# A new table of places for the backward recurrence of a memory transformer on one core

## The chip, the cores and the metric

The kernel runs on one core of one Trainium2 chip. The metric is the time of one execution on the device in microseconds (us). Three runs of the kernel before gave 2830.5, 2833.98 and 2844.75 us; the median, 2833.98, is the time to compare with. The engines are named as in the profile: PE (TensorE, matmuls; PEld is its weight load), DVE (VectorE), ACT (ScalarE), POOL (GpSimd) and SP, on whose queue all transfers of the stage concerned are issued.

## The reference

The forward pass is a layer norm, then the sum of the input, an attention whose memory of 8 rows is carried from one segment of 32 tokens to the next, and an MLP with a squared ReLU. The kernel computes the output and the gradients of all ten tensors for a given gradient of the output.

```python
B, S, Dm = (1, 2048, 512)
H, Dh = (32, 128)
M, seg = (8, 32)
...
for s in range(n_seg):
    xs = x[:, s * seg_len:(s + 1) * seg_len, :].copy()
    h = jnp.concatenate([mem, xs], axis=1)
    q = jnp.einsum('btd,dhe->bhte', h, Wq)
    k = jnp.einsum('btd,dhe->bhte', h, Wk)
    v = jnp.einsum('btd,dhe->bhte', h, Wv)
    scores = jnp.einsum('bhqe,bhke->bhqk', q, k) * scale
    scores = jnp.where(mask[None, None], scores, -1000000000.0)
    p = _softmax(scores, axis=-1)
    o = jnp.einsum('bhqk,bhke->bhqe', p, v)
    o = jnp.einsum('bhte,hed->btd', o, Wo)
    mem = o[:, :M, :].copy()
    outs.append(o[:, M:, :])
...
return x + _A_ref(xn, A_mem0, A_Wq, A_Wk, A_Wv, A_Wo, A_seg_len) + _B_ref(xn, B_w1, B_b1, B_w2, B_b2)
...
_out, _vjp = jax.vjp(_f, A_x, A_mem0, A_Wq, A_Wk, A_Wv, A_Wo, B_w1, B_b1, B_w2, B_b2)
_grads = _vjp(grad_out)
return (_out0, *[jnp.asarray(_g) for _g in _grads])
```

There are 64 segments, each of which needs the memory of the one before; in the backward pass each needs the gradient of the memory of the one after.

## The kernel before

The program has the stages forward recurrence, MLP, backward recurrence (the second recurrence, L1705 to L2078) and weight gradients (L2162). Only the second recurrence is touched. It walks the 64 segments from the last to the first, in 16 blocks of four; the segments of a block are called 3, 2, 1 and 0, and are done in that order.

**One segment's chain** (`chain`, L1920). The gradient of the memory comes from R_A, the sum for this segment's input rows. R_A is evicted from PSUM in two halves (L1980 states them, L763 is an eviction on DVE, L765 one on ACT; in the trace R_A is an XN of 128x256, f32). The matmul **gm** (L1992) picks the memory rows out of it, and a copy on DVE (L1995) puts them into the matrix gT. Then **gO**, the projection by the output weights (L873, four parts gO00, gO01, gO10, gO11), its eviction, its transposes **gOT** (L759) and their eviction, and **dP** (L1937), the gradient of the probabilities, in two halves. On DVE the softmax backward follows, for each half four operations (L1958, L1960, L1961, L1963) and transposes (L1967, L1968). Small copies fill block-diagonal matrices from its results (L999; BDA, BDB and XK in the trace), on ACT, DVE or POOL. With these PE does the **bd** matmuls (L983; bd2, bd1 and bd0 for v, k and q, each in two halves), each half is evicted (L765 or L763, into XK), transposed on DVE (L856), and multiplied by the weights (**dR2, dR1, dR0**, L1777, four steps each) into R_A for the segment before. The evicted gradients, dN, also go to memory (S_GN, three stores of 256 KB per segment); dN2 and dN0 share one buffer, so the next one is evicted after the store has read it.

**Filler.** Between the steps of the chain PE does work of neighbouring blocks that does not hang on the chain: `l_pre` (L1788) prepares the next block's local part (gL and dp, and pre.dg at L939, and a softmax on DVE, L1760 to L1765), and `l_post` (L1826) finishes the last block's: post.own (L1864), post.mm (L1877) and dRL (24 steps of L1777, with XN as input). gNat (L2013) are transposes of gT after a block is done.

**What sets the order.** Nothing is scheduled when the kernel is built. `_Beat.run` (L573) pops the operations from a heap as soon as those they depend on are out. The key is a number from a table plus a fixed beat for each block; the remainder of the number by 4 names the engine, for the copies that several engines can do:

```python
x = own[1 if o.blk == 0 else 2 if o.blk == self.last else 0][o.slot]
e = ("PE", "ACT", "DVE", "POOL")[x % 4] if len(o.cost) > 1 else next(iter(o.cost))
heapq.heappush(heap, (self.beat * o.blk + x // 4, o.idx, e))
...
_, i, e = heapq.heappop(heap)
seq.append((self.ops[i], e))
```

There are three tables in `_BWD` (L197): for the 14 middle blocks, for the first and for the last block. Each engine, and SP's queue, does its instructions in the order in which they come off the heap. A place is only an order; a transfer or an engine that is late makes those behind it wait.

Of the kernel before, what the change touches and what calls it, by code (L numbers as in the profile page):

```python
# [205 lines left out]
        -546000, -2857200, -480000, -481200, -46343678, 1958400, 3563600, 3428400, 3358800, -39445799, -3474280,  # L206
        -1361679, 2911440, -5698598, 6099600, 4994800, 2060400, 541200, 4580802, 7385202, 7385602, 8326802, 8824402,
        9103200, 9060400, 12611600, 12610400, 6769762, -57689959, -4334000, -3086798, -8438400, -12837600, -319597,
        -13471197, -16186000, 938000, 7771520, 7770320, 7974082, -12147880, -36138158, 8458960, 7771680, -8353800,
        -31747319, 8462400, -36193079, 9695640, -50492597, -69540277, -42304997, -47596277, 5526803, -19093437,  # L210
        -6835677, -4532037, 8168480, -52982319, 8492560, -35859039, 8101002, 8275242, 9959080, -11536760, 2676160,
        -6802360, -5640120, 8030522, 8029322, 8640522, 11057002, 11480802, 11054602, 11479602, 11169682, 11053402,
        11052202, 11166082, 12529242, 13047722, 11577282, -53185477, -47912717, -46746037, -35873437, -26574079,
        -41158999, -3076599, -21554757, 11212360, -21629439, -6090039, 11539522, 7252481, -6895997, -8092680,
        -17924919, 12833482, 13066282, 12876240, 12875040, 12828880, 12873840, 14037400, -57547477, -18138439,
        -21536557, -24487719, 11602322, -46193917, 11601122, -40852157, -10002840, 13779282, -43878718, 11390242,
        -39385558, -10128439, -12102397, -45351999, -12199997, -9629117, 12830080, 13828081, -1848078, -8506838,
        12332320, 12331120, 12380240, 12380240, -37160200, 14192521, 14713641, 2556960, -5265118, 1378880, -58560038,
        9791040, -36825960, 23496720, -26575120, 3544040, -30169437, 10715403, 14217080, -2427160, -21531640,
        -24941080, -26533360, -965320, -9348360, -4744280, -2117080, -9645557, -4299440, -4982320, -4689600, -3734720,  # L220
        -45051079, 1432880, -190760, 143640, 170960, -12251559, 4149840, 4316040, 4314840, 4313640, -444838, -2435878,
        4726002, 5218242, -314198, 6272960, 6271760, 6140240, 6422880, -13898000, 15057720, 15056520, -78482159,
        15704400, -31640798, 16583800, 15669280, 15668080, -31651159, 16441160, 4105522, 17918400, -44856717,
        -49497237, 12097443, 14069203, 15760843, -13303037, -24924477, 14658563, -1036080, -12120519, 16517640,
        -12171479, -19164078, 16333722, 18497320, 18496120, 18374600, 18373400, -16882000, -7618398, 19291482,
        8963202, -1006558, 7859002, -10244638, -8975838, 19549882, -19454878, -2022158, -22659278, 4534722, 17929402,
        -18420838, -4276997, 10220123, -15301237, 16219523, -28146359, -10193797, -48781357, -18599357, 18309560,
        -23528479, -13879038, -7373558, -10161077, -9652838, 19720960, -4986318, 19557922, 16324922, 20802000,
        20800800, 21247800, 21246600, 20708240, -48823239, -5933437, -20262439, -26219437, -700039, -18122837,
        -19469237, -21622759, 18592960, 19820441, -17140839, -38326879, -20258439, -24316917, -15836677, -9607317,  # L230
        10993321, -19470397, 20806200, -9618559, -2440598, 10800642, 20664920, 20663720, 21187560, 19381040, 9514760,
        -31648438, -51401599, 21992720, 6632762, 21999880, 19977762, 14024000, 11239960, 23859600, -49781320,
        -27474160, 11856363, 5703803, -13820320, -23800120, 22382040, 20342520, -21640039, 22438800, -18114918,
        22528840, 22438280, 22171720, 8096121, 22699840, -20694919, 23625560, 12662283, -30947157, 14340323,
        -31376917, 12732363, 20788683, -20774837, -9932197, 22519320, -5755239, 22616720, -4144719, 13732122,
        21493322, 24284480, 24289280, 24279680, 24286880, 710240, 12368682, 12608882, 16282482, 23172642, 23649362,
        18415762, 23257962, 21492122, 23472122, 23038122, 23036922, 20708242, 23650562, 24117602, -10181877, 15361043,
        -45284197, -5213277, -28628559, 11584403, -18779559, 16282521, 24308840, 4772161, 11541603, 7885001, 21513123,
        9730121, 24352920, 4695441, 22456642, 23126042, 25675960, 25672360, 26009600, 25617680, 8765280, 12337841,
        -14024677, -21028397, -14720079, 5575883, 23280602, 23322362, 14584721, 24369440, 22963802, 8381161, 8379961,  # L240
        2859121, 18921401, 25701003, 23965202, 13830203, 23373882, 25671160, 10999201, 16305242, 25052002, 26008400,
        25669960, 25668760, 25868480, 16157920, 12553281, 10227922, 26094160, -18057118, 26108720, -31954518,
        26951160, -20195520, 14049520, -22449760, -3877280, 26096323, 15608603, 21197560, 10032720, 26241320,
        26237720, -19414239, 26281240, 26771362, -19806600, 26280720, 26279520, 11529081, 26799680, 20066961,
        28507720, 12895563, 10136643, 21059483, 21141563, 26591123, 7004643, 22356883, 6439723, 22656520, 11629001,
        24627920, 20068161, 25696402, 25018762, 28743680, 28743680, 28742480, 29779680, -42422640, 11044042, 16305082,
        27921522, 27538322, 29068802, 24650882, 6776522, 26190882, 16313322, 19375402, 11190962, 29320522, 16274042,
        11238882, 25372323, 20587803, 9815123, -48383117, 19292523, 3013201, 11530761, 19745083, 29055200, -32040879,
        16256721, -18660637, -21773197, -4282917, 30337920, 13860201, 29354602, 29326002, 31079640, 29877760,
        32090560, 31697440, 12144000, 13033521, -14471839, 1277843, -14338079, -9612957, -10090479, -21864637,  # L250
        -21541959, 30830320, 22919881, 3768961, 13666041, 1722803, 27275443, 18430083, 14474482, 20602681, 7341881,
        31157240, 13824001, 29362442, 19648322, 32088160, 32091760, 32086960, 32088160, 12960080, 26104721, 4714882,
# [129 lines left out]
_BWD_BEAT = 6498400  # L382
# [1842 lines left out]
```

## Time and profile before

| what | us |
| --- | --- |
| median of three runs | 2833.98 |
| lowest and highest run | 2830.5 and 2844.75 |
| span of the profiled execution | 2847.0 |
| first block of the second recurrence, 1209.5 to 1285.0 | 75.5 |
| fourteen middle blocks, 1285.0 to 2208.0 | 923.0, or 65.9 each |
| last block, 2208.2 to 2274.7 | 66.5 |
| tail, up to the weight gradients | 17.0 |

The profiled execution has one number here, its span from the first instruction to the last; that span is 13 us above the median and 2 us above the highest of the three runs. Parts of it are therefore to be compared with the span, and not with the median. The stretches of the stage are read off the trace where the first gO of a block starts.

A row of waits reads "engine line <- releaser: us in all, times, longest". A row of the timeline gives start, length, engine, line, operation, output and input, count, and in brackets the idle time before it with what ended it. In a row of a table of stretches there stand the busy time and the number of instructions of each engine, PE's granted clock (1.00 is full), the share of busy transfer engines and GB/s.

### The profile page before, as it was taken

The numbers are of one execution on the slowest core, as the hardware profiler recorded it, in microseconds if no ns is written. First come the engines' busy times: TensorE is split into PE (matmuls) and PEld (weight loads), VectorE is DVE, ScalarE is ACT, GpSimd is POOL, SyncE is SP. The second block draws the span as 40 slices with busy tenths as digits, with TensorE's granted clock in tenths as the row PEclk, the third lists the DMA queues.
The fourth block names the chain that finished last, engine by engine and source line by source line (L and its number), as shares of the span: only waits on it lengthen the run. The fifth ranks groups of instructions, "written<-read, shape, count | busy, mean of one in ns | idle before, by whom it ended". The sixth has DMA issues, their size and how long they took to land.

```text
span 2847.0 us, 114405 instructions
## 1 busy us (share of the span) xinstructions
PE 2708.2 (95%) x47681; PEld 1558.6 (55%) x47681; DVE 1630.3 (57%) x4762; ACT 1191.0 (42%) x2804; POOL 935.3 (33%) x2605
## 2 busy tenths in 40 slices
PE   9999999999999999889998999999999899999999
PEld 7665556566565565655555555555555544444444
DVE  5555666666666567776676666666676502232322
ACT  4334445555555455565554555554554400000000
POOL 1103233223333233344454444444444301111211
PEclk9999999999999999999999999999999999999999
DMA  7648677787777764568898898888888799788861
GB/s 222 208 151 239 190 195 199 211 211 203 208 206 205 194 192 161 147 163 227 224 235 217 219 228 237 221 224 223 227 220 210 224 353 295 229 254 268 254 184 42
DMA packets 556394, 606.28 MB, mean 213 GB/s; under 512 B 228145, under 2 KB 357442, under 8 KB 553826
## 3 DMA queue, kind: packets, MB, share of 16 engines
q1 hardware_dynamic: 540706, 544.88, 70.0%
q0 software_dynamic: 15168, 54.08, 6.1%
q8 instruction: 374, 6.13, 0.9%
q14 instruction: 146, 1.20, 0.1%
HBM read 290.14 MB, written 272.12 MB: 197 GB/s over the span
## 4 chain that ended last, share of the span: by engine, by line
PE 62%; DVE 12%; issue 11%; DMA 7%; ACT 3%; POOL 2%; SPq 2%; DVEq 0%; POOLq 0%; ACTq 0%
PE ps L873 16%; PE ps L2162 10%; PE ps L1777 8%; PE ps L983 5%; PE ps L759 4%; PE ps L1442 4%; PE ps_h L1183 3%; DMA S_GN<-XK 3%; PE ps L1655 3%; PE ps_B L1211 2%; PE ps_gxb L1211 2%; DVE maskA L1963 1%; SPq L819 1%; DVE XN L856 1%; ACT XK L765 1%
## 5 line engine op out<-in xcount | busy, mean ns | idle before, releaser
L873 PE MATMUL ps<-WA,PA 128*32 128x512 bf16 x6144 | 370.8, 380 | 5.3 <-DVE PA L1603 3.8
L2162 PE MATMUL ps<-WA,WB 128*128 128x512 bf16 x1536 | 332.3, 379 | 0.6 <-DVE gwo L763 0.6
L1777 PE MATMUL ps<-WA,XK 128*32 128x512 bf16 x5120 | 315.6, 381 | 9.7 <-DVE XK L856 6.2
L873 PEld LDWEIGHTS <-PA 128*32 128x32 bf16 x8192 | 208.3, 96 | 196.4 <-issue 11.3
L2162 PEld LDWEIGHTS <-WB 128*128 128x128 bf16 x1896 | 185.5, 98 | 224.5 <-issue 0.8
L999 POOL COPY BDA<-PB 32x128 bf16<-32x128 bf16 x468 | 134.9, 288 | 487.3 <-DVE PLp L1571 182.0
L763 DVE CAST gwo<-ps 128x512 bf16<-128x512 f32 x64 | 40.0, 682 | 400.3 <-PE ps L2162 268.3
L765 ACT CAST gwo<-ps 128x512 bf16<-128x512 f32 x64 | 33.1, 599 | 517.2 <-PE ps L2162 357.9
L765 ACT CAST XK<-ps 128x512 bf16<-128x512 f32 x330 | 189.5, 585 | 106.0 <-PE ps L983 61.3
L1777 PEld LDWEIGHTS <-XK 128*32 128x32 bf16 x5120 | 124.6, 97 | 144.9 <-DVE XK L856 36.3
L1777 PE MATMUL ps<-WA,XN 128*32 128x512 bf16 x2560 | 166.1, 385 | 5.9 <-DVE XN L856 5.4
L2173 POOL DMA_DIRECT2D out_dram<-gwo x96 | 71.4, 751 | 295.9 <-ACT gwo L765 264.9
L763 DVE COPY XN<-ps 128x512 bf16<-128x512 bf16 (+1 forms) x146 | 65.7, 450 | 156.5 <-PE ps L759 104.5
L765 ACT CAST XA<-ps 128x512 bf16<-128x512 f32 x141 | 82.8, 587 | 141.7 <-PE ps L873 121.3
L999 ACT COPY BDA<-PB 32x128 bf16<-32x128 bf16 x452 | 133.4, 295 | 14.3 <-DVE PB L1967 2.0
L1442 PE MATMUL ps<-WB,OT 128*32 128x256 bf16 x4096 | 130.7, 275 | 6.7 <-DVE mxA L1577 3.9
L1655 PE MATMUL ps<-XA 128*128 128x512 bf16 x448 | 133.3, 382 | 1.9 <-issue 1.9
L873 PE MATMUL ps<-WB,PA 128*32 128x512 bf16 x2048 | 126.2, 384 | 6.4 <-issue 5.2
L765 ACT COPY XN<-ps 128x256 f32<-128x256 f32 (+2 forms) x158 | 73.9, 480 | 136.5 <-DVE XN L763 75.3
L983 PEld LDWEIGHTS <-XK 128*128 128x128 bf16 x1536 | 94.2, 98 | 61.5 <-POOL XK L999 26.1
L856 DVE STREAM_TRANSPOSE XK<-XK 128x256 f32<-128x256 f32 x256 | 108.7, 436 | 31.8 <-ACT XK L765 28.2
L1005 POOL COPY BDA<-XA 32x256 bf16<-32x256 bf16 x256 | 105.8, 413 | 59.7 <-PE ps L983 34.3
(309 smaller groups left out, 5555.5 us busy)
## 6 DMA issues: line engine op xcount, KB each, us to landing
S_GN<-XK SPq DMA_DIRECT2D x192, 256.0 KB
WA<-S_GN SPq DMA_DIRECT2D x160, 256.0 KB
S_K<-kN SPq DMA_DIRECT2D x64, 256.0 KB
S_Q<-qN SPq DMA_DIRECT2D x64, 256.0 KB
S_V<-vN SPq DMA_DIRECT2D x64, 256.0 KB
S_ON<-oN SPq DMA_DIRECT2D x64, 256.0 KB
XA<-S_Q SPq DMA_DIRECT2D x64, 256.0 KB
XA<-S_K SPq DMA_DIRECT2D x64, 256.0 KB
```

The lines of the kernel that those rows point to most:

```text
L759: nc.tensor.transpose(ps_ap, in_ap, ident[base:base + k, base:base + k])
L765: nc.scalar.copy(out, in_)
L856: self.plan.add({"DVE": 0.36}, lambda e, x=x: nc.vector.transpose(dst[:, x, :, :].rearrange("p i c r -> p (i c r)").bitcast(F32).rearrange ...
L873: nc.tensor.matmul(bk()[32 * j:32 * (j + 1), :], lhsT=win(dc), rhs=Wt(dc, c0), start=(dc == 0), stop=(dc == DC - 1), tile_position=(0, 32 ...
L983: nc.tensor.matmul(bv()[:, n * P:(n + 1) * P], lhsT=B_[:, i, :, :].rearrange("p j k -> p (j k)"), rhs=X[:, i, :], start=(y == 0 and n == 0 ...
L999: self.plan.add({"ACT": 0.31, "DVE": 0.2, "POOL": 0.31}, lambda e, j=j: {"ACT": nc.scalar.copy, "DVE": nc.vector.tensor_copy, "POOL": nc.g ...
L1005: self.plan.add(cost or {"ACT": 0.4, "DVE": 0.27, "POOL": 0.42}, lambda e, j=j: {"ACT": nc.scalar.copy, "DVE": nc.vector.tensor_copy, "POO ...
L1211: nc.tensor.matmul(bk()[:], lhsT=src[z][:, fc, rc * P:(rc + 1) * P], rhs=Wt[:, fc, :], start=(fc == 0 and first), stop=(fc == FC - 1))
L1442: nc.tensor.matmul(bk()[32 * t:32 * (t + 1), :], lhsT=tq(OTt, i, j), rhs=Wo[:, JQ * i + j, h * HB:(h + 1) * HB], start=(i == 0 and j < 2), ...
L1655: A(pe(0.217, "f", 0.11), lambda e, c=c, z=z, x=x: nc.tensor.matmul(bks[x]()[:], lhsT=anT[x][:, c, :], rhs=sx[z][:], start=(c == 0), stop= ...
L1777: nc.tensor.matmul(bk()[32 * j:32 * (j + 1), :], lhsT=tq(XT, i, j), rhs=wtf(t, i, j), start=(first and i == 0), stop=(last and i == NI - 1 ...
L2162: nc.tensor.matmul(bks[n]()[:], lhsT=HNc[:, rc, dc * P:(dc + 1) * P], rhs=half_of(gns[y], hf), start=(y == 0), stop=(y == NRC - 1))
```

## The change

Numbers of the three tables of `_BWD` are replaced: 550 of the 724 for the middle blocks and all of the first block's 618 and the last block's 561. The beat goes from 6498400 to 6498399. No code and no table of the forward recurrence is touched. The new numbers come from a search whose replay serves the packets of all transfers in the order of issue. What shows in a program is another order on the five engines and other engines for some copies: of the copies, evictions and casts, DVE has 1462 (1655 before), ACT 2641 (2464) and POOL 2233 (2217). Matmuls and transfers are the same ones. The new file is one line shorter, so each line behind the table has a number lower by one.

```diff
@@ -203,183 +203,182 @@
         11817202, 10472800, 15851602, -17692400, -106800, -10764000, 216000, -12492400, 3623200, 6284000, -528797,
-        -546000, -2857200, -480000, -481200, -46343678, 1958400, 3563600, 3428400, 3358800, -39445799, -3474280,
...
-_BWD_BEAT = 6498400
+_BWD_BEAT = 6498399
```

Three places show what moves. The first is DVE in segment 3 of a middle block, from the end of the first half's softmax backward to the first fill of BDB after the second half's (maskA is the result, PB its transpose). Before:

```order
L1963 SCALAR_TENSOR_TENSOR maskA<-XA 128x160
L1967 STREAM_TRANSPOSE PB<-maskA 128x128
L1958 TENSOR_TENSOR XA<-ps,XA 128x160
L1960 TENSOR_REDUCE brA<-XA 128x4
L1961 TENSOR_TENSOR XA<-ps,brA 128x160
L1963 SCALAR_TENSOR_TENSOR maskA<-XA 128x160
L1966 COPY PB<-maskA 128x4x8
L1968 STREAM_TRANSPOSE PB<-PB 128x128
L999 COPY BDB<-maskA 32x4x32
```

And with the change:

```order
L1962 SCALAR_TENSOR_TENSOR maskA<-XA 128x160
L1965 COPY PB<-maskA 128x4x8
L1966 STREAM_TRANSPOSE PB<-maskA 128x128
L1967 STREAM_TRANSPOSE PB<-PB 128x128
L855 STREAM_TRANSPOSE XN_2675<-XK_2673 128x256
L1957 TENSOR_TENSOR XA<-ps,XA 128x160
L1959 TENSOR_REDUCE brA<-XA 128x4
L1960 TENSOR_TENSOR XA<-ps,brA 128x160
L1962 SCALAR_TENSOR_TENSOR maskA<-XA 128x160
L1966 STREAM_TRANSPOSE PB<-maskA 128x128
L998 COPY BDB<-maskA 32x4x32 x2
```

The copy and transpose of the first half (L1966 and L1968 of before) moved ahead of the second half's softmax, the transpose at L1967 for the second half ahead of the fills, and DVE fills two parts of BDB instead of one. On PE in the same segment, dR2's first two steps went ahead of the second dP, its last two and bd0's first half between the two halves of bd1, and the transposes of gNat behind the first dP. The eviction of gNat went from DVE to ACT.

The second place is PE around gm, in segment 1 of a middle block. XN is here the input of dRL (filler), XK_2673 that of dR0 (the chain), PA the gT that gO reads. Before:

```order
L1777 LDWEIGHTS XN_2678
L1777 MATMUL ps<-WA,XN_2678 32x512
L1992 MATMUL ps<-sel_97,XN_2677 32x8 x16
L1777 LDWEIGHTS XN_2678
L1777 MATMUL ps<-WA,XN_2678 32x512
```

With the change:

```order
L1776 LDWEIGHTS XK_2673
L1776 MATMUL ps<-WA,XK_2673 32x512
L1991 MATMUL ps<-sel_97,XN_2677 32x8 x16
L872 LDWEIGHTS PA
L872 MATMUL ps<-WB,PA 32x512
```

The filler before gm and behind it is gone in this segment and in segment 2: gm stands right behind the last step of dR0, and gO right behind gm. In segments 3 and 0 there is still filler ahead of gm. Both evictions of R_A are ACT's in every segment now; before, DVE did 45 of them.

The third place is SP's queue, from late in segment 1 to early in segment 0 of a middle block; XK_2673 is the buffer of dN, S_V, S_VM and S_VL are loaded transposed, XA, S_Q and S_K belong to the loads of q and k. Before:

```order
L819 DMA S_GN<-XK_2673 128x1024
L819 DMA XA<-S_Q 128x1024
L1784 DMA_TRANSPOSE XK_2672<-S_VM 128x8x128
L819 DMA XA<-S_K 128x1024
L819 DMA S_GN<-XK_2673 128x1024
L1784 DMA_TRANSPOSE XA<-S_V 128x8x128
L1784 DMA_TRANSPOSE XK_2672<-S_VL 128x8x128
L819 DMA S_RL<-XN_2682 128x512
L819 DMA S_GON<-XA 128x1024
L819 DMA S_GN<-XK_2673 128x1024
```

With the change:

```order
L818 DMA XA<-S_Q 128x1024
L818 DMA XA<-S_K 128x1024
L818 DMA S_GN<-XK_2673 128x1024
L1783 DMA_TRANSPOSE XA<-S_V 128x8x128
L818 DMA S_GN<-XK_2673 128x1024
L818 DMA S_R<-XN_2677 128x512
L818 DMA S_RL<-XN_2682 128x512
L818 DMA S_GON<-XA 128x1024
L818 DMA S_GN<-XK_2673 128x1024
```

Before, the first S_GN row is dN1 of segment 1, the second dN0 of segment 1 and the third dN2 of segment 0, which needs the buffer of that dN0. With the change dN0 is stored first and dN1 behind it; the transposed load of S_VM went into segment 2 and that of S_VL further away.

338 rows, old and new, of the table _BWD are left out of this document.

## The prediction

> **What bounds the kernel now.** First the page: the span, and who is busy in it.
>
> ```profile
> span 2847.0 us, 114405 instructions
> PE 2708.2 (95%) x47681; PEld 1558.6 (55%) x47681; DVE 1630.3 (57%) x4762; ACT 1191.0 (42%) x2804; POOL 935.3 (33%) x2605
> ```
>
> PE is busy for 95% of the span, so a change of order alone can win at most PE's idle time, and only that of the stage it touches. The change touches the second recurrence. The table by stretches gives its four parts: first block, fourteen middle blocks, last block, and the tail up to the weight gradients.
>
> ```profile
> core 0: us, PE busy (x) PEld busy (x) DVE busy (x) ACT busy (x) POOL busy (x), PEclk, DMA share, GB/s
> 1209.50:1285.00 75.50, 67.22 (x1488) 43.28 (x1480) 52.40 (x142) 44.00 (x91) 33.78 (x102) 1.00 0.63 167
> 1285.00:2208.00 923.00, 857.87 (x19422) 493.82 (x19424) 610.82 (x1828) 491.05 (x1182) 437.50 (x1358) 0.99 0.87 224
> 2208.20:2274.70 66.50, 59.63 (x1239) 33.77 (x1232) 40.22 (x126) 31.64 (x78) 28.03 (x89) 0.97 0.73 214
> 2274.70:2291.70 17.00, 13.00 (x203) 6.69 (x201) 2.35 (x5) 2.23 (x4) 0.00 (x0) 0.90 0.91 304
> ```
>
> Span less PE's busy time: 8.3 us idle in the first block, 65.1 in the middle (4.65 per block), 6.9 in the last, 4.0 in the tail: 84 us in all. DVE, ACT and POOL are busy for 66%, 53% and 47% of the middle, so none of them is the bound; what counts is how late one result comes. The waits of PE in the middle say which:
>
> ```profile
> engine line waited for: us in total, times, longest us
> PE ps L983 <- DVE BDB L999: 13.0, 15, 1.3
> PE ps L1937 <- ACT XN L765: 7.0, 6, 2.4
> PE ps L873 <- issue: 5.5, 6, 1.4
> PE ps L1777 <- DVE XN L856: 5.4, 6, 1.9
> PE ps L983 <- issue: 4.3, 4, 2.1
> PE ps L983 <- POOL XK L999: 4.3, 13, 0.3
> PE ps L1777 <- DVE XK L856: 3.4, 16, 0.5
> ...
> PE ps L1992 <- ACT XN L765: 0.4, 1, 0.4
> ```
>
> Some 20 of the 65 us are "issue" (the two rows above and smaller ones): pauses that wait for nothing that is shown, which I take as untouched. About 36 us wait on an engine and can be moved. Four rows carry my sum: 13.0, 7.0, 5.4 and 4.3.
>
> **The change part by part.** No instruction of PE and no transfer is added or removed; about 190 copies go from DVE to ACT. So every term is a wait that goes, shrinks or appears.
>
> *The 13.0 us, once per block, in segment 3.* PE stands before the second half of the bd1 matmuls until DVE has filled BDB:
>
> ```profile
> 1687.52 0.86 PE L1877 MATMUL ps<-XN,XN 128*32 128x128 bf16 x32
> 1687.75 0.28 DVE L1958 TENSOR_TENSOR XA<-ps,XA 128x160 f32<-128x160 f32 x1
> 1688.54 0.39 PE L983 MATMUL ps<-XA,BDB 128*128 128x128 bf16 x4
> 1688.76 0.39 PE L983 MATMUL ps<-bqLN,XK 128*128 128x128 bf16 x4
> 1689.71 0.18 DVE L999 COPY BDB<-maskA 32x128 bf16<-32x128 bf16 x1
> 1690.04 0.38 PE L983 MATMUL ps<-XA,BDB 128*128 128x128 bf16 x4 [0.90 <-DVE BDB L999]
> ```
>
> DVE's second softmax half starts at 1687.75 and its fill ends at 1689.89. What decides is how much PE work lies between the first dP and this matmul. Four matmuls of a bd take 0.22 (the two groups that start at 1688.54 and 1688.76), so a half of bd takes 0.45; 16 of post.mm take 0.43 (half of 0.86); 16 of dR2 take 1.04 (row below). Before, what lies there is gOT1, bd2's second half, post.own, dP 1, dR2 (four steps), post.mm twice, bd1's first half and 0.22 of its second. Changed, all this and besides it bd0's first half (0.45) and the transposes of gNat (four matmuls, 0.22 by the same row): 0.7 more, against a mean wait of 13.0/14 = 0.93. DVE does not get there earlier: the eviction of gNat leaves it, a transpose and one more fill of BDB (0.18) come in, as the rows of the order show. Bounds: +2.5 (only the extra fill counts, 14 x 0.18) and -13.0. I take 14 x 0.7 = **-9.8**. What is late next there is bd0's second half, behind POOL.
>
> *The 7.0 us.* One of these six waits, in segment 0, with the ACT work that leads to it, and the row of all such waits of ACT:
>
> ```profile
> 1799.22 1.07 ACT L765 CAST XK<-ps 128x512 bf16<-128x512 f32 x2 [2.62 <-DMA S_GN<-XK]
> 1800.18 0.60 ACT L765 COPY XN<-ps 128x512 bf16<-128x512 bf16 x1
> 1800.84 0.28 PE L1937 MATMUL ps<-XA,XN 128*32 128x40 bf16 x16 [1.48 <-ACT XN L765]
> ...
> ACT XK L765 <- DMA S_GN<-XK: 27.1, 20, 3.1
> ```
>
> ACT stood for 2.62 us before an eviction into XK, because the store of the segment before (S_GN) was still reading that buffer; the eviction of gOT queued behind it, and PE behind that. In the change the store in question goes out ahead of the other store and of two transposed loads. Bounds: +2.6 (one more wait like the one shown) and -7.0; I take three quarters, **-5.3**. The 5.4 us at L1777 <- DVE XN L856 stand behind DVE's transpose of what such an eviction leaves, mostly in segment 2; there l_post's dRL steps now lie around the second dP as cover: 0 to -5.4, half, **-2.7**. The 4.3 us at L983 <- POOL: fewer fills of segment 3 stand behind POOL's copies of V (L1911); 0 to -4.3, half, **-2.1**. Together -19.9.
>
> *New: R_A uncovered.* In segments 2 and 1 no PE work is left between the last dR0 and gm (the rows of the order in the section above). R_A must first be evicted. Two places show it, covered and uncovered:
>
> ```profile
> 1266.76 0.65 ACT L765 COPY XN<-ps 128x256 f32<-128x256 f32 x2 [1.73 <-PE ps L1777]
> 1266.85 0.69 DVE L1763 TENSOR_TENSOR XN<-ps,brL 128x512 f32<-128x512 f32 x1
> 1267.19 0.59 PE L1992 MATMUL ps<-sel,XN 128*32 128x8 f32 x32 [0.46 <-ACT XN L765]
> ...
> 1727.88 1.04 PE L1777 MATMUL ps<-WA,XN 128*32 128x512 bf16 x16
> 1728.10 0.42 DVE L763 COPY XN<-ps 128x256 f32<-128x256 f32 x1 [1.61 <-PE ps L1777]
> 1728.56 0.37 ACT L765 COPY XN<-ps 128x256 f32<-128x256 f32 x1 [2.55 <-DVE XN L763]
> 1728.98 0.44 PE L1992 MATMUL ps<-sel,XN 128*32 128x8 f32 x32
> ```
>
> Below, in segment 1 of a middle block, 16 matmuls of l_post (1.04) cover both halves of the eviction and gm does not wait. Above, in the first block, nothing covers and PE idles 0.46. The first block's other gm waited up to 0.9 (rows further down). Two per block, 28 in all: bounds 28 x 0.2 = 5.6 (if ACT is free at once and the first half suffices for the first matmuls) and 28 x 0.9 = 25.2. I take the row itself, 28 x 0.46 = **+12.9**.
>
> Both halves now go to ACT, and the rows show that this loses nothing: DVE's half ended at 1728.52, ACT's began at 1728.56. If the two could run side by side, taking DVE away would cost one more 0.37 at each of the 28 uncovered places, 10.4 us; by the rows it costs 0. The Trainium skill ("PSUM — Partial Sum Buffer", section "PSUM bank collisions raise a hardware error ⚠️") says that software has to keep two engines apart on the same bank, which would put the halves one behind the other whoever copies; the trace agrees, with 0.04 us between them.
>
> *New: less between gO and its transposes.* In segments 1 and 0, gOT0 now follows gO10 directly; gO11 comes after it.
>
> ```profile
> 1332.89 1.85 PE ps L873 x32
> ...
> 1730.69 0.59 ACT L765 CAST XA<-ps 128x512 bf16<-128x512 f32 x1 [1.76 <-PE ps L873]
> ```
>
> A quarter of gO takes 1.85/4 = 0.46; the eviction before the transposes 0.59, so PE lacks 0.13 and what the hand-over takes, 0.2 by my estimate (0.04 lies between the two halves of R_A above). Bounds 0.1 and 0.4; 28 x 0.2 = **+5.6**. In segment 0, dR1's third step now precedes bd0's second half and needs a transpose that DVE does behind one softmax step of l_pre (0.69 at L1763): 0 to 0.69, nearest to the middle since two steps of dR1 (1.04, as for dR2) still cover: 14 x 0.3 = **+4.2**. Together +22.7.
>
> Middle blocks: -19.9 + 22.7 = +2.8.
>
> *First and last block* have their own tables.
>
> ```profile
> PE ps L1992 <- ACT XN L765: 1.4, 2, 0.9
> PE ps L983 <- DVE BDB L999: 1.0, 2, 0.8
> ...
> PE ps L1992 <- DVE XN L763: 0.9, 1, 0.9
> ...
> PE ps L1937 <- ACT XN L765: 2.8, 1, 2.8
> PE ps L1877 <- DMA XN<-S_DSL: 2.4, 2, 1.9
> ```
>
> The first three are the first block's. There gm gets l_pre's and l_post's work as cover in segment 0, and gO and dP move up: of 1.4 + 1.0 + 0.9 = 3.3 and the small ones of its 8.3 us I take -4 (0 to -6). In the last block l_post's dRL steps move in beside segment 0, which covers the 2.8 us: -3 (0 to -5). The 2.4 us in the tail wait for a load behind the last store and stay.
>
> **Sum**: 2.8 - 4 - 3 = -4.2 us. The profiled execution spans 2847.0 us, 13 above the median of 2834.0 (runs 2830.5 to 2844.75), so its own result would be 2842.8; carried to the median, **2829.8**.
>
> **Rivals.** *A: the covers hold and the new gaps are small.* All four rows go (13.0 + 7.0 + 5.4 + 4.3 = 29.7), gm costs 0.2 a time, gOT 0.1, dR1 nothing: 5.6 + 2.8 = 8.4. With -7 for the ends: -28.3, 2805.7. For it: 13 us of the gain are one regular wait, and the cover fits. Against: the filler that pays for it stood before gm.
>
> *B: slower, through ACT's queue.* ACT carries both halves of R_A in every segment and gets twelve copies more per block; where one eviction of another chain (0.59) stands ahead of R_A, gm waits 0.46 + 0.59 = 1.05. That is 28 x 0.59 = 16.5 beyond the forecast, and the 5.3 taken off dP's wait are lost with it, since dP waits for ACT too: -4.2 + 21.8 = +17.6, 2851.6. Up to a wait of 0.61 at gm the kernel gains (4.2/28 = 0.15 above 0.46); from 0.93 on it is slower by what can be measured (14.2 + 4.2 - 5.3 = 13.1, 0.47 a time). For it: the first block's 0.9. Against: ACT is busy for 53% only.
>
> *C: the transfers do not keep the order of issue*, so that the new places of the S_GN stores, chosen for such an order, gain nothing: the 5.3 and 2.7 fall away, -4.2 + 8.0 = +3.8, 2837.8. For it: the row of 27.1 us shows 20 waits of ACT for stores of one size, issued by one queue, at places that differ from block to block, up to 3.1. The Trainium skill speaks for C: "DMA: Bandwidth & Descriptors", section "Two DMAs through the same engine are not ordered", has it that descriptors of one queue start in order but are pipelined, and that nothing orders transfers across the 16 engines. No row here shows two transfers overtaking each other.
>
> **How the numbers follow.** Forecast 0.38, A 0.30, C 0.12, B 0.20. About 0.5% (14.2 us: 2819.8 and 2848.2) is what a measurement of this kernel can tell from no change. Faster: A's 0.28 and 0.08 of the forecast's lower side, 0.36. Slower: B's 0.17 and 0.04 of the forecast's and C's upper side, 0.21. Same: 0.43. The forecast's own range is 2817 to 2843; to hold 8 in 10 the range runs into A and B, from 2802 to 2852.
>
> **What would show it.** In the profile after: "L983 <- DVE BDB" of the middle near 3 (right) or above 8 (wrong); "L1992 <- ACT XN" about 13, below 6 for A, above 25 for B; "L1937 <- ACT XN" below 3, or still 7 for C; "L759 <- ACT XA" new with about 5; idle of PE in the first block about 4 and in the last about 4. The prediction fails if the pauses named "issue" change, or if a late load (GON, loaded late for l_post) stops PE for whole microseconds in every block.

## The result, and the profile after

The changed kernel takes 2800.18 us (median of five runs, 2798.07 to 2812.79), the kernel before 2837.44 us (five runs, 2830.5 to 2844.75): a ratio of 0.9866, with a 95% interval from 0.9835 to 0.9897. It is faster by 1.3%, where the forecast was 2829.8 and no difference that can be told; 2800.18 lies just below the range of the forecast, 2802 to 2852.

The head of the page of the profiled execution after the change:

```profile
span 2811.0 us, 114204 instructions
PE 2701.3 (96%) x47681; PEld 1555.9 (55%) x47681; DVE 1532.6 (55%) x4569; ACT 1259.3 (45%) x2981; POOL 937.5 (33%) x2621
```

The span is 36.0 us shorter. To see where, the same stretch is cut out of both: from the first gm of segment 3 of the second block to that of the last block, which are fourteen blocks. The rows of the table by stretches are, in this order, of before, of the change, and of the change profiled a second time (columns: stretch, length, busy time of PE, PEld, DVE, ACT and POOL with counts, PE's clock, share of busy transfer engines, GB/s):

```profile
1299.70:2222.60 922.90, 858.47 (x19436) 494.26 (x19432) 611.23 (x1826) 491.20 (x1184) 437.50 (x1358) 0.99 0.87 224
1293.70:2186.60 892.90, 851.38 (x19360) 493.82 (x19356) 523.88 (x1655) 551.73 (x1345) 438.29 (x1364) 0.99 0.94 232
1286.40:2174.30 887.90, 849.34 (x19363) 493.96 (x19359) 523.66 (x1655) 551.72 (x1345) 438.24 (x1364) 1.00 0.94 233
```

The fourteen blocks are shorter by 30.0 us (922.9 to 892.9), 2.1 us per block. PE is idle in them for 41.5 us instead of 64.4, and its busy time is 7.1 us less, but this stretch also holds 76 matmuls fewer with the change, since some filler lies on the other side of the cut. The whole stage, from the last matmuls of one line late in the forward recurrence (L1554 before, L1553 after) to the end of the tail, has the same number in both:

```profile
1171.40:2291.70 1120.30, 1030.25 (x22976) 605.61 (x22969) 738.73 (x2165) 590.98 (x1389) 516.01 (x1585) 0.99 0.84 218
1165.30:2256.00 1090.70, 1026.18 (x22976) 604.97 (x22969) 640.42 (x1972) 658.30 (x1566) 518.68 (x1602) 0.99 0.90 225
```

It is shorter by 29.6 us, of which PE's busy time gives 4.1. The other 6 us of the span lie ahead of the stage, where nothing was changed: it starts at 1171.4 us before and 1165.3 after. First and last block give nothing, as the same table shows for the first block, the last and the tail of the change (75.5, 66.5 and 17.0 us before):

```profile
1200.80:1274.90 74.10, 69.87 (x1549) 44.40 (x1548) 47.67 (x131) 45.82 (x96) 35.78 (x111) 0.99 0.64 172
...
2171.00:2237.00 66.00, 62.03 (x1243) 34.18 (x1239) 34.48 (x113) 35.16 (x84) 29.55 (x96) 0.97 0.77 231
2237.00:2256.00 19.00, 11.98 (x206) 5.80 (x206) 1.78 (x4) 2.15 (x4) 0.00 (x0) 0.83 0.82 241
```

The waits of PE in the stretch of the change, and the row of ACT's waits for the stores of dN:

```profile
engine line waited for: us in total, times, longest us
PE ps L1991 <- ACT XN L764: 13.4, 28, 0.5
PE ps L1991 <- issue: 8.5, 7, 2.5
PE ps L872 <- issue: 3.4, 4, 1.9
PE ps L872 <- DVE PA L1994: 3.2, 18, 0.2
...
PE ps L1776 <- DVE XK L855: 2.1, 3, 1.3
...
ACT XK L764 <- DMA S_GN<-XK: 6.4, 7, 2.1
```

The wait of bd1 for BDB (13.0, or 12.2 in this stretch) is gone, and so is that of dP for ACT (7.0). gm (L1991) waits 28 times, 0.48 each. ACT's wait for S_GN fell from 27.1 to 6.4.

What had been in the trace of before, and was overlooked, is in segment 3 of a middle block. The timeline of before shows the segment's first dP, and POOL's copy of V beside the last step of the softmax backward of the first half; then follow, of the change, the first dP, that step of both halves, the fill of BDB, the matmul that needs it, and the copy:

```profile
1684.14 0.28 PE L1937 MATMUL ps<-XA,XN 128*32 128x40 bf16 x16
1686.20 1.03 POOL L1911 COPY XA<-XA 128x1024 bf16<-128x1024 bf16 x1
1686.47 0.94 DVE L1963 SCALAR_TENSOR_TENSOR maskA<-XA 128x160 bf16<-128x160 f32 x1
...
1664.11 0.28 PE L1936 MATMUL ps<-XA,XN 128*32 128x40 bf16 x16
1665.85 0.33 DVE L1962 SCALAR_TENSOR_TENSOR maskA<-XA 128x160 bf16<-128x160 f32 x1
1668.75 0.33 DVE L1962 SCALAR_TENSOR_TENSOR maskA<-XA 128x160 bf16<-128x160 f32 x1
1669.41 0.34 DVE L998 COPY BDB<-maskA 32x128 bf16<-32x128 bf16 x2
1670.16 0.39 PE L982 MATMUL ps<-XA,BDB 128*128 128x128 bf16 x4
1674.83 1.03 POOL L1910 COPY XA<-XA 128x1024 bf16<-128x1024 bf16 x1
```

The same instruction took 0.94 us beside the copy and takes 0.33 without it. The change has the copy 14.9 us after the segment's first gO, where it stood 4.9 us after it. That is not what took the wait away, though. The second half's fill ends 5.64 us after the first dP with the change (1664.11 to 1669.75) and ended 5.75 after it before (1684.14 to 1689.89): the step is shorter by 0.61, but DVE now has more to do ahead of the fill. It is PE that comes later, 6.05 us after the first dP, where it stood ready after 5.0 (1690.04 less the wait of 0.90). The medians of the fourteen blocks are the same: fill 5.76 before and 5.65 with the change, PE ready 5.01 and 6.05.

### The profile page after: what moved, and what is told of

Read it like the earlier page. It is cut to its first block, busy times and chain, and to the rows that moved or that the text cites. A ratio compares the mean times of both kernels' runs of the same rounds, so it can differ in the third digit from the quotient of the medians.

```text
span 2811.0 us, 114204 instructions
## 1 busy us (share of the span) xinstructions
PE 2701.3 (96%) x47681; PEld 1555.9 (55%) x47681; DVE 1532.6 (55%) x4569; ACT 1259.3 (45%) x2981; POOL 937.5 (33%) x2621
## 4 chain that ended last, share of the span: by engine, by line
PE 63%; issue 8%; DMA 4%; DVE 4%; ACT 2%; POOL 1%; SPq 0%; DVEq 0%; POOLq 0%; ACTq 0%
PE ps L872 14%; PE ps L1776 14%; PE ps L2161 12%; PE ps L982 7%; PE ps L758 4%; PE ps L1441 3%; PE ps L1654 2%; PE ps L1991 1%; PE ps L1876 1%; PE ps L938 1%; ACT XN L764 1%; PE ps L1936 1%; DMA S_GN<-XK 1%; DMA WA<-S_GN 1%; PE ps L1598 1%
## 5 line engine op out<-in xcount | busy, mean ns | idle before, releaser
L872 PE MATMUL ps<-WA,PA 128*32 128x512 bf16 x6144 | 371.1, 381 | 4.8 <-DVE PA L1602 3.8
L998 POOL COPY BDA<-PB 32x128 bf16<-32x128 bf16 x546 | 157.4, 288 | 490.3 <-DVE PLp L1570 198.1
L872 PEld LDWEIGHTS <-PA 128*32 128x32 bf16 x8192 | 206.2, 97 | 190.1 <-DVE PA L1994 12.0
L1776 PE MATMUL ps<-WA,XK 128*32 128x512 bf16 x5120 | 306.5, 382 | 4.0 <-DVE XK L855 3.9
L764 ACT CAST XK<-ps 128x512 bf16<-128x512 f32 x379 | 210.6, 589 | 80.5 <-PE ps L982 67.6
L1776 PE MATMUL ps<-WA,XN 128*32 128x512 bf16 x2560 | 173.3, 381 | 3.7 <-DVE XN L855 3.4
L764 ACT COPY XN<-ps 128x256 f32<-128x256 f32 (+2 forms) x229 | 102.2, 475 | 128.2 <-PE ps L1776 125.3
L872 PE MATMUL ps<-WB,PA 128*32 128x512 bf16 x2048 | 135.4, 389 | 8.0 <-issue 3.6
L1441 PEld LDWEIGHTS <-OT 128*32 128x32 bf16 x4096 | 102.2, 97 | 35.3 <-DVE OT L855 19.4
L1004 POOL COPY XK<-XH 32x64 bf16<-32x64 bf16 x256 | 59.5, 232 | 182.0 <-PE ps L982 171.1
```

What stands on the lines that cost most here:

```text
L764: nc.scalar.copy(out, in_)
L872: nc.tensor.matmul(bk()[32 * j:32 * (j + 1), :], lhsT=win(dc), rhs=Wt(dc, c0), start=(dc == 0), stop=(dc == DC - 1), tile_position=(0, 32 ...
L998: self.plan.add({"ACT": 0.31, "DVE": 0.2, "POOL": 0.31}, lambda e, j=j: {"ACT": nc.scalar.copy, "DVE": nc.vector.tensor_copy, "POOL": nc.g ...
L1004: self.plan.add(cost or {"ACT": 0.4, "DVE": 0.27, "POOL": 0.42}, lambda e, j=j: {"ACT": nc.scalar.copy, "DVE": nc.vector.tensor_copy, "POO ...
L1441: nc.tensor.matmul(bk()[32 * t:32 * (t + 1), :], lhsT=tq(OTt, i, j), rhs=Wo[:, JQ * i + j, h * HB:(h + 1) * HB], start=(i == 0 and j < 2), ...
L1776: nc.tensor.matmul(bk()[32 * j:32 * (j + 1), :], lhsT=tq(XT, i, j), rhs=wtf(t, i, j), start=(first and i == 0), stop=(last and i == NI - 1 ...
```

## The experiments

All times are compared with runs of the kernel before on the same chip. The stretch of fourteen blocks is cut as above. It holds pauses of PE that wait for nothing shown ("issue"), which differ from one execution to the next; the last column leaves them out, and so compares profiles better than the length does. What it still holds is the clock: now and then PE was granted half of it for 3.4 us, as in this row of before (the fields as above):

```profile
1535.90:1539.30 3.40, 3.40 (x88) 1.96 (x77) 2.95 (x11) 2.30 (x7) 2.71 (x7) 0.50 0.50 115
```

The stretch holds three of these before and three with the change, one in the second profile of the change, in e1 and in e3, four in e2 and e12, three in e6, e9 and e11, and none in e4, e5, e8 and e13. Each can cost up to 1.7 us, so a few us in the last column are no difference.

| kernel | ratio to before, interval | 14 blocks, us | pauses, us | blocks less pauses, us |
| --- | --- | --- | --- | --- |
| before | 1 | 922.9 | 20.9 | 902.0 |
| the change | 0.9866 (0.9835 to 0.9897) | 892.9 | 17.9 | 875.0 |
| r: the change again | 0.986 (0.9833 to 0.9886) | 887.9 | 12.6 | 875.3 |
| e1: new order, old engines | 1.0245 (1.0225 to 1.0265) | 980.9 | 0.8 | 980.1 |
| e2: old order, new engines | 1.014 (1.0107 to 1.0172) | 955.9 | 21.5 | 934.4 |
| e4: store swapped in the change | 0.9869 (0.9848 to 0.989) | 891.7 | 13.0 | 878.7 |
| e5: bd1 early in the change | 0.9875 (0.9855 to 0.9895) | 891.2 | 5.1 | 886.1 |
| e3: gm covered in the change | 0.987 (0.9847 to 0.9892) | 886.8 | 14.8 | 872.0 |
| e8: half of R_A on DVE in the change | 0.985 (0.9828 to 0.9873) | 888.1 | 12.8 | 875.3 |
| e6: store early in before | 0.9974 (0.9959 to 0.9989) | 921.1 | 21.5 | 899.6 |
| e9: POOL's copies late in before | 0.9989 (0.9975 to 1.0003) | 918.9 | 16.9 | 902.0 |
| e11: e6 and e9 together | 0.9955 (0.9939 to 0.997) | 913.6 | 20.7 | 892.9 |
| e12: e11, one load later | 0.9921 (0.9898 to 0.9945) | 909.3 | 19.9 | 889.4 |
| e13: e3 and a store earlier | 0.9854 (0.9828 to 0.988) | 880.9 | 10.8 | 870.1 |

**e1 and e2: order or engines?** Each number of the table carries a place and an engine. The two were crossed:

```diff
-t = new
+t = [[n // 4 * 4 + o % 4 for n, o in zip(*p)] for p in zip(new, old)]    (e1)
+t = [[o // 4 * 4 + n % 4 for n, o in zip(*p)] for p in zip(new, old)]    (e2)
```

> The order of the change, with the engines of the kernel before for every copy. Theory O (the order of PE, DVE and the transfers brings the gain; the engines of copies are a detail): at least two thirds of the gain stays, 2798 to 2815 us. Theory E (the gain needs the copies on ACT, since DVE carries the softmax chain): under a third stays, 2826 to 2850 us, with waits for DVE back in the middle blocks.

> The order of before, with the engines of the change. Theory O: no gain or a loss, 2832 to 2860 us. Theory E: a gain of at least 10 us, below 2827 us, and the wait of bd1 for BDB below 5 us in the middle blocks (13.0 before).

Neither theory holds: e1 is 2.4% slower than before, e2 1.4%. The largest waits of PE in the fourteen blocks, of e1 and then of e2:

```profile
PE ps L939 <- DVE XH L1818: 21.8, 14, 1.6
PE ps L1777 <- DVE PB L1966: 16.3, 13, 1.4
PE ps L1777 <- DVE XN L856: 15.7, 27, 0.7
...
PE ps L983 <- ACT XK L999: 37.8, 54, 1.7
PE ps L983 <- DVE XK L999: 8.6, 14, 0.6
```

In e1 DVE does the copies of before in an order made for fewer of them, and PE waits for DVE's steps; in e2 PE waits 54 times for a fill that ACT does. That the copies in between are what delays these steps is argued from the rows and not shown by a run of its own. The two halves of this table can't be priced apart.

**e4: one store back.** In the change, segment 1's store of dN0 is put behind that of dN1 (SP's queue, a middle block):

```diff
 L819 DMA XA<-S_K 128x1024
-L819 DMA S_GN<-XK_2673 128x1024
-L1784 DMA_TRANSPOSE XA<-S_V 128x8x128
-L819 DMA S_GN<-XK_2673 128x1024
+L1784 DMA_TRANSPOSE XA<-S_V 128x8x128
+L819 DMA S_GN<-XK_2673 128x1024 x2
```

> The change with one transfer moved in each middle block: the store of dN0 of segment 1 goes out behind that of dN1, as before the change. Theory T (the place of this store on SP's queue took the wait of the second dP of segment 0 away): the wait of dP for ACT, 0 in the middle blocks of the change, comes back with 3 to 7 us, and the time rises by 4 to 10 us. Rival (the 7.0 us went because dP comes later on PE or less was in flight): the wait stays below 2 us and the time within 3 us of the change.

```profile
PE ps L1992 <- ACT XN L765: 13.8, 29, 0.5
...
PE ps L1937 <- ACT XN L765: 4.5, 5, 1.2
```

These rows of PE's waits in e4 show the wait of dP back with 4.5 us, as theory T has it, and the blocks less pauses are 3.4 us longer than in the second profile of the change. The time did not rise by the 4 to 10 us of theory T; it can't be told from the change's (0.9869 against 0.9866), as the rival has it.

**e5: less cover for bd1.** In segment 3 of the change, dR2's last two steps and bd0's first half go behind bd1's second half (the rows of PE, each standing for its group of matmuls):

```diff
 L1877 MATMUL ps<-XN_2682,XN_2681 32x128
+L983 MATMUL ps<-XA,BDB 128x128
 L1777 MATMUL ps<-WA,XN_2675 32x512
 L983 MATMUL ps<-XA,BDA 128x128
-L983 MATMUL ps<-XA,BDB 128x128
```

> The change with PE's order in segment 3 of the middle blocks partly undone: the second half of bd1 stands again straight behind post.mm, ahead of dR2's last two steps and of bd0's first half (1.35 us of work). Theory P (cover decides, the fills come at the same time): PE waits for BDB again by 1.1 to 1.2 us per block, 14 to 17 us in the waits, and the time rises by 14 to 20 us. Rival (the fills of BDB come earlier by themselves with the new order of DVE and ACT): the wait is below 6 us and the time rises by less than 8 us.

```profile
PE ps L1992 <- ACT XN L765: 13.4, 28, 0.5
PE ps L983 <- DVE BDB L999: 10.7, 12, 0.9
```

The waits of PE in e5: the wait for BDB is back with 10.7 us, below theory P's 14 to 17 and above the rival's 6. The fill still ends 5.65 us after the first dP, and PE is ready after 4.90 (medians): without the cover the wait is there again, so in the change the cover is what removes it. The blocks less pauses are 10.8 us longer than in the change, but the time is up by only 0.09 to 0.15% against the two measurements of the change, which is within the intervals, not the 14 to 20 us of theory P and under the rival's 8. In this profile the pauses are 5.1 us, where the change had 17.9 and 12.6. Whether a wait of PE takes pauses away was not settled.

**r, e3 and e8: the change again, gm covered, and half of R_A on DVE.**

> The changed kernel itself once more, as the base for the three others on the same chip: 2795 to 2812 us. It also tells how large the pauses of PE that wait for nothing are from one execution to the next: if they are the program's, the same places again with 16 to 20 us in the middle blocks as before (17.9); if they are of the moment, other places or another sum.

The two profiles of the change differ by 5.0 us in the fourteen blocks, and by 0.3 us once the pauses are left out. So the pauses are of the moment in their size; most of their places are the program's (last section).

In e3 three steps of filler go ahead of gm in every middle block; in segment 1 it is one step of dRL, in segment 2 one of dRL and this one of gL (four matmuls, shown once):

```diff
 L1777 MATMUL ps<-WA,XN_2675 32x512
-L873 MATMUL ps<-WB,PB 32x512
 L983 MATMUL ps<-bkLN,XK_2672 128x128
...
 L1777 MATMUL ps<-WA,XK_2673 32x512
+L873 MATMUL ps<-WB,PB 32x512
 L1992 MATMUL ps<-sel_97,XN_2677 32x8 x16
```

> The change with filler put back ahead of gm in the middle blocks: in segment 2 one step of gL and one of dRL (0.65 us), in segment 1 one step of dRL (0.22 us), each taken from a later place in the same segment where PE's inputs had been ready for 0.4 to 1.0 us. Theory G (the uncovered gm costs its 0.46 us and the drain before it, 28 times): the wait of gm for ACT falls from 13.4 to below 6 us, and the time falls by 6 to 10 us against the change. Rival (PE is bound elsewhere in these segments, the wait only moves): the wait falls as much, and others rise by as much; time within 3 us.

```profile
PE ps L1777 <- DVE XK L856: 8.4, 21, 1.0
...
PE ps L1992 <- ACT XN L765: 4.4, 16, 0.5
```

The wait of gm fell from 13.4 to 4.4, as both theories say, and 8.4 us appeared before dR0 (2.1 in the change, 3.3 in its second profile). The time did not move (2801.35 against 2801.47 us on the same chip): the rival holds. Here a gap at gm isn't a loss of its own; the filler that could close it was closing another one.

In e8 the first half of R_A is DVE's in segments 2 and 1:

```diff
 L856 STREAM_TRANSPOSE XK_2673<-XK_2673 128x256 x4
+L763 COPY XN_2677<-ps 128x256
 L1995 CAST PA<-ps 128x2x8 x2
```

> The change with the first half of R_A evicted by DVE in segments 2 and 1 of the middle blocks, the second by ACT as now. Theory S (two engines take turns on one bank of PSUM): gm waits as long as in the change, 12 to 16 us in all, time within 4 us. Rival (the halves run side by side): the wait of gm falls by a third or more (28 times 0.2 us or so), the time by 5 to 10 us.

```profile
PE ps L1992 <- DVE XN L763: 14.9, 28, 0.5
```

This row of PE's waits in e8 is the answer: gm waits as long, now by DVE's name, and theory S holds. In all 28 places ACT's half starts 0.03 us after DVE's has ended, so the two never run side by side; the pair takes 0.83 us, against 0.65 where ACT does both. (Of all 128 such evictions in the trace of the change, two are still DVE's, in the first block.) In the rows of the prediction ACT's half is released by DVE's, so the program itself has one wait for the other; whether the bank would allow both at once was not tried.

**e6: the store early, in the kernel before.** The load of S_VM goes behind the store of dN0:

```diff
 L819 DMA XA<-S_Q 128x1024
-L1784 DMA_TRANSPOSE XK_2672<-S_VM 128x8x128
 L819 DMA XA<-S_K 128x1024
 L819 DMA S_GN<-XK_2673 128x1024
+L1784 DMA_TRANSPOSE XK_2672<-S_VM 128x8x128
```

> The kernel before with one transfer moved per middle block: the transposed load of S_VM goes out behind the store of dN0 of segment 1, not two places ahead of it. Theory T (queue ahead of the store makes dP wait in segment 0): the wait of dP for ACT falls from 7.0 us to below 3 in the middle blocks, the time by 4 to 10 us. Rival C (the order of issue does not decide): the wait stays at 5 or more, the time within 4 us of before.

```profile
PE ps L983 <- DVE BDB L999: 11.7, 13, 1.2
PE ps L1777 <- DVE XN L856: 8.7, 7, 2.1
```

In the waits of e6 that of dP, 7.0 us before, has no row any more, and the time is 0.26% lower, 7 us: theory T, and rival C falls: here the order of issue on one queue decides when PE gets on. The row of L1777 <- DVE XN, 5.4 before, is 3.3 us longer.

**e9: POOL's copies late, in the kernel before.** On POOL, the two copies of V go behind the segment's last fill in segments 3 and 2 (here segment 3), and on SP the next load of V goes behind the next store of dN1:

```diff
-L1911 COPY XA<-XA 128x32x32
-L1914 COPY XA<-XK_2672 128x32x8
 L999 COPY BDB<-maskA 32x4x32
 L999 COPY BDA<-PB 32x4x32 x2
...
 L999 COPY XK_2672<-PB 32x4x32 x3
+L1911 COPY XA<-XA 128x32x32
+L1914 COPY XA<-XK_2672 128x32x8
```

> The kernel before with POOL's two copies of V for the next segment (1.04 and 0.39 us) moved, in segments 3 and 2 of the middle blocks, from ahead of the fills to behind the last fill of the segment, and the transposed loads that follow them on SP moved as far back. Nothing else. Theory V (in before, the big copy on POOL runs beside the last step of the first softmax half on DVE, which then takes 0.94 us where it takes 0.33 alone, and this is what makes BDB late): that step takes 0.33 again, the wait of bd1 for BDB falls from 13.0 us to below 6 in the middle blocks, and the time falls by 7 to 14 us. Rival K (the step is slow for another reason, or PE's cover alone decides): the step stays above 0.7 or the wait above 9, and the time within 4 us.

The groups of DVE by line in the fourteen blocks give the mean of the softmax's last step, in ns behind the total: of before, of the change, of e9. Then the waits of PE in e9, and two of ACT:

```profile
L1963 DVE SCALAR_TENSOR_TENSOR maskA<-XA 128x160 bf16<-128x160 f32 x112 | 48.0, 429 | 9.6 <-DVE XA L1961 0.5
L1962 DVE SCALAR_TENSOR_TENSOR maskA<-XA 128x160 bf16<-128x160 f32 x112 | 36.5, 326 | 11.7
L1963 DVE SCALAR_TENSOR_TENSOR maskA<-XA 128x160 bf16<-128x160 f32 x112 | 37.9, 339 | 9.6 <-DVE XA L1961 0.5
...
PE ps L1937 <- ACT XN L765: 14.4, 14, 2.9
PE ps L1777 <- ACT dLN L765: 9.5, 11, 1.8
...
PE ps L983 <- DVE BDB L999: 2.7, 9, 0.6
...
ACT XK L765 <- DMA S_GN<-XK: 23.6, 20, 3.5
ACT dLN L765 <- DMA S_GNL<-dLN: 19.9, 9, 3.0
```

The mechanism is as theory V says: the step's mean falls from 429 to 339 ns, and the wait for BDB from 12.2 to 2.7 with PE's order untouched. (After the first dP the fill ends 0.34 us earlier than before, 5.42, and PE is ready 0.19 later, 5.20; medians.) The time is not as theory V says (0.9989): the wait of dP doubled to 14.4, and a new one of 9.5 came, of an eviction into dLN that waits for the store S_GNL, which the moved load now stands ahead of. That transfers ate the gain is what e11 and e12 test.

**e11 and e12: the causes put together.** e11 has the edits of e6 and e9. e12 moves the load of V for segment 1 behind the stores it stood ahead of:

```diff
-L1784 DMA_TRANSPOSE XA<-S_V 128x8x128
 L819 DMA S_GNL<-dLN 128x1024
 L819 DMA XH_2684<-S_PLL 128x512
...
 L819 DMA S_R<-XN_2677 128x512
 L819 DMA S_GON<-XA 128x1024
+L1784 DMA_TRANSPOSE XA<-S_V 128x8x128
```

> The kernel before with the moves of e9 and that of e6 (the load of S_VM behind the store of dN0). If the two causes add up: 13 to 21 us below before, 2816 to 2824 us at before = 2837, and the waits for BDB and of dP together below 8 us (20.0 before). If the chain is held by something else as well, the second move adds under 3 us to the first.

> As e11, but the transposed load of V for segment 1 goes out four transfers later on SP, behind the stores that it held up in e9 and e11 (there PE waited 9.5 and 10.1 us for an eviction into dLN, which waited for the store S_GNL). Theory Q (what the first move of e9 won was eaten by transfers put in the way of others): the wait for dLN falls below 3 us, and the time falls to 2812 to 2822 us at before = 2840 (18 to 28 us below before). Rival (something else takes its place, as in e9): under 4 us below e11, 2826 us or more.

The waits of PE, three rows of e11 and three of e12:

```profile
PE ps L1777 <- ACT dLN L765: 10.1, 10, 2.2
...
PE ps L983 <- DVE BDB L999: 3.1, 11, 0.6
PE ps L1937 <- ACT XN L765: 2.1, 4, 1.0
...
PE ps L1937 <- ACT XN L765: 3.5, 3, 2.3
PE ps L983 <- DVE BDB L999: 2.5, 9, 0.6
...
PE ps L1777 <- ACT dLN L765: 0.6, 1, 0.6
```

e11 is 0.45% below before, 13 us: the two causes add up to the least that was expected of that, and more than each alone (0.26% and 0.11%). In e12 the wait for dLN is down to 0.6, and the time 0.79% below, 22 us, as theory Q has it. A few moves on POOL and SP, with no move on PE, DVE or ACT, give more than half of what the whole new table gives (0.79% of 1.34%, with an interval from 0.55% to 1.02%).

**e13: a version ahead of the change?** e3, with segment 2's store of dN2 ahead of two others on SP:

```diff
 L819 DMA S_GN<-XK_2673 128x1024
-L819 DMA S_GNL<-dLN 128x1024
-L819 DMA S_R<-XN_2677 128x512
-L819 DMA S_GN<-XK_2673 128x1024
+L819 DMA S_GN<-XK_2673 128x1024
+L819 DMA S_R<-XN_2677 128x512
+L819 DMA S_GNL<-dLN 128x1024
```

> The change with the filler ahead of gm as in e3, and on SP the store of dN2 of segment 2 two places earlier, ahead of two other stores. In e3 PE then waited 8.4 us for a transpose behind an eviction that waits for this store. Theory Q (stores of dN are the next bound): that wait falls below 3 us, ACT's wait for S_GN from 16.0 to below 8, and the time is 4 to 10 us below the change (ratio to before 0.9835 to 0.985). Rival (transfers are full as a whole, some other one is late in its place): ratio 0.985 to 0.988, as e3.

```profile
PE ps L1777 <- DVE XK L856: 7.6, 18, 2.3
...
ACT XK L765 <- DMA S_GN<-XK: 10.6, 10, 3.0
```

The wait before dR0 stayed (7.6 of 8.4), ACT's for S_GN fell to 10.6 (16.0 in e3). 2796.94 us, 0.9854, lies in the rival's range and can't be told from the change. The blocks less pauses are the shortest of all, 870.1, but 1.9 us less than in e3 is no more than the one half-clock stretch that e3 has and e13 has not.

## Why the prediction was wrong

**The step that failed** is the sum of the middle blocks, -19.9 + 22.7 = +2.8. It let the old waits go in part only, and set against them three new ones in full. Of these two hardly came, and the third, gm's, came as forecast but was no loss that filler could win back (e3). In the rows of PE's waits on engines and transfers the fourteen blocks have 35.1 us before and 19.5 with the change, -15.6 where the sum had +2.8. For the whole stage the forecast was -4.2 and the measured change -29.6: 16.4 are such waits (57.8 to 41.4), 4.7 pauses (22.8 to 18.1), 4.1 PE's busy time, and 4.4 gaps too short to have a row. So 13.2 us stand where the sum took nothing. Which moves of the table gave these 13.2 us no run shows.

**The wait for BDB, forecast -9.8, measured -13.0.** The mechanism, PE's cover, was right (e5), and the size too small: the cover grew by 1.04 us and not by 0.7. In part, by the timeline, this is because work cut in pieces takes longer: the 32 matmuls of dR2 took 1.73 us in one piece (1685.79 to 1687.52 before); with the change 16 of them take 0.98 (1665.32 to 1666.30). "DVE does not get there earlier" came out nearly right, 0.11 us, but not for the reason given. It counted DVE's instructions in the order and not how long one lasts. One of them lasted 0.94 us (the median; 0.86 to 1.16) instead of 0.33 in every middle block, since POOL's copy of V ran beside it. The change took the copy away, which paid for what DVE got to do ahead of the fill; with the copy still there the fill would end at some 6.26 us (5.65 + 0.61, an estimate), 0.2 after PE is ready. In the order of before, e9's moves alone take the wait to 2.7. The mean of that line, 429 ns above, was in the trace of before, beside those of two steps of like size (groups of DVE by line, before):

```profile
L1961 DVE TENSOR_TENSOR XA<-ps,brA 128x160 f32<-128x160 f32 x112 | 34.7, 310 | 2.4
L1958 DVE TENSOR_TENSOR XA<-ps,XA 128x160 f32<-128x160 f32 x112 | 34.1, 304 | 21.2 <-PE ps L1937 20.5 <-ACT XK L765 0.6
```

The Trainium skill ("SBUF — State Buffer", section "🔬 SBUF: two separate sides") says that VectorE and GpSimd share one port pair, held for a whole instruction by a VectorE operation with two SBUF inputs against a GpSimd one that reads SBUF. The step has two SBUF inputs (L1963 reads XA and the probabilities), and the steps ahead of it, which read PSUM and one SBUF input, kept their 0.28 to 0.33 us; the trace agrees with the rule. In the order of before either of the two would suffice for most of the wait (PE's cover of 6.05 us outlasts a fill at 5.76), so they don't add up.

**The waits that hang on S_GN, -5.3 and -2.7, measured -7.0 for dP and -5.4 for dR2 in the fourteen blocks (a wait of 2.3 us of this kind stands just ahead of them); the small one at L983 <- POOL, -2.1, measured -4.3.** For dP the mechanism was right: e6 takes its wait away with one transfer, e4 brings 4.5 back. For the other two no run isolates it. The shares taken, three quarters and a half, were too cautious. Rival C falls.

**gm uncovered, +12.9, measured 13.4 in the waits.** The size was right, and its place in the sum wrong: e3 closes two thirds of it and gains nothing, because the chain then waits at dR0. It was entered as a cost of its own, while what its filler now covers in other places was entered only where the table of waits has a row. The smaller entries of that kind were too large as well: +5.6 for gOT against 0.6 (1.0 in the second profile), and +4.2 for dR1, which has no row. One of 3.2 us, of gO for the copy into gT (L872 <- DVE PA, 0.3 before), was not forecast.

**What no row of waits shows.** The prediction counted PE's idle time alone as what an order can win. Over the whole stage PE's busy time fell by 4.1 us with the same number of matmuls, and with six half-clock stretches in both. A hold-up is in part counted as busy, because a matmul's row lasts longer than its turn (0.38 us in the mean at L1777, where the 32 of dR2 above follow each other every 0.05): the pause at row 65474 of the change's trace (last section) is 1.04 us of idle time and 1.42 from start to start.

**First and last block, -4 and -3, measured -1.4 and +1.5.** Their waits changed names, and the tail got one of 4.4 us for a load (L1876 <- DMA XN<-S_DSL) where it had 2.4.

**The sum.** Middle blocks: forecast +2.8, measured -30.0, of which 3.0 (20.9 to 17.9) are pauses. Rival A, with 2805.7 us, was the nearest; it has its gain from the right rows, and the condition it names, small new gaps, isn't what happened: the gap at gm is there, and closing it wins nothing. That it came so near is in part luck, since it counts none of the 13.2 us that have no row.

What stays open: e12 reaches 889.4 us less pauses, the second profile of the change 875.3. Of these 14.1 us, 1.0 are waits that have a row (22.8 and 21.8), 4.1 gaps too short for one, and 9.0 PE's busy time (858.3 and 849.3). Up to 5.1 of the 9.0 can be the clock (four half-clock stretches in e12, one in that profile), and some 80 matmuls more lie in e12's stretch. By the times of the runs the change stays 0.6% ahead of e12 (0.986 and 0.9921). Which moves of the table give that was not tried.

## What to carry to other kernels

Before an order is priced, compare the mean of each line with lines of like size: one that is a third longer, as here, may be held up by a neighbour, and a change of order moves neighbours. Where filler is only moved about, a gap closed at one place can open at another, as in e3, so count the chain and not the gaps. When a wait goes, compare when each of its two sides arrives, before and after: the side that seems to explain it may not have moved. When a wait is taken away and the time stays, look at what the transfers on the same queue now stand ahead of.

## What the hardware showed that was not expected

In the trace of before, 33 of the 112 executions of L1963 in the middle blocks (1285.0 to 2208.0) ran beside POOL's copy at L1911 and took 0.69 us in the mean, against 0.33 for the others. In 27 of the 33 the step ended 0.18 us after the copy did, whatever part of it they shared. Steps that read PSUM (L1958, L1961) and stream transposes (L856) beside the same copy took no longer than alone (0.28, 0.32 and 0.44). In e2 a small copy from SBUF to SBUF (L1966, 0.17 alone) took 0.60 beside it, thirteen times, and each ended 0.03 us after POOL's copy.

Most pauses of PE that wait for nothing have fixed places in PE's row of instructions. Counted in the trace of the change, four of them stand at its rows 65474, 68290, 71106 and 76738, and in its second profile at 65356, 68172, 70988 and 76620: steps of 2816 or twice that, which is 11 times 256, and the same four places but for 118 records. How long a pause is differs: 1.4, 2.3, 1.6 and 1.8 us (from start to start) the first time, 1.5, 1.1, 1.9 and 0.8 the second. Of the 17 pauses of the change 12 stand at the same places in its second profile, and 16 at rows that leave the same remainder, 194, when divided by 256. What PE waits for there is not seen in the trace.

With the change the transfer engines are busy for 94% of the fourteen blocks (87% before), at 232 GB/s, and PE for 95% of them. Which of the two would be the next bound no run shows.
